# Memory attention and bilinear FFN: three groups of small-tile matmuls made neighbours, and the next-but-one batch's loads moved into the output stage

## The chip, the core and the metric

The kernel runs on one core of a Trainium2 chip. The metric is device time in microseconds (us). The kernel before takes 522.99 us (median of three runs, 522.94 to 523.03). Its profiled execution took 522.87 us, of which the span that the trace covers is 520.7 us. All times below, unless said otherwise, count from the start of that span.

## The reference

Eight batches, eight heads, 576 tokens, head dimension 64, 32 memories. `q` and `k` come multiplied by 200. Attention goes through the memories, and its output feeds a bilinear feed-forward network:

```python
a = phi - np.max(phi, axis=2, keepdims=True)          # max over the tokens
a = np.exp(a); a = a / (np.sum(a, axis=2, keepdims=True) + 1e-09)
k_m = np.einsum('bhsm,bhsd->bhmd', a, k)
v_m = np.einsum('bhsm,bhsd->bhmd', a, v)
scores = scale * np.matmul(q, k_m.transpose(0, 1, 3, 2))
scores = scores - np.max(scores, axis=-1, keepdims=True)
attn = np.exp(scores); attn = attn / (np.sum(attn, axis=-1, keepdims=True) + 1e-09)
x = np.matmul(attn, v_m)                               # heads side by side: 4608 x 512
h = (x @ w1) * (x @ w2) @ w3                           # 512 -> 1024 -> 1024
out = h @ w_out                                        # 1024 -> 512
```

## The kernel before, in words

Batch by batch (b = 0 to 7) the kernel works through a row of small steps. The order of all five engines is written out by hand: one token per step in three tables, `FIRST` for b = 0, `SECOND` for b = 1 and `BATCH` for b = 2 to 7. Each engine executes its share of the steps in the table's order and waits where data or a buffer isn't there yet; nothing overtakes on an engine. Two stages make up a batch: the a·b stage, with 16 units, and the out stage, with 14.

Tokens that matter here, with the line and the engine:

- `A`, `a`, `g`: one unit of a·b. `A` is 12 matmuls 128 x 288 on tiles 128\*128 (L596, TensorE = PE) into two PSUM banks of a ring of four ("ab" banks); `a` copies one bank (L605, ScalarE = ACT), `g` multiplies the other by it (L608, VectorE = DVE). fp32 values are split into a high and a low part, so each product is three matmuls.
- `M0` to `M3`: 16 matmuls each with 64\*32 tiles (L346) that multiply the values' memories into `w1` and `w2`; `Mh` (L357, ACT) and `Ml` (L365, DVE) split the result. M0 and M1 of batch b+1 are done in the out stage of b, M2 and M3 in the a·b stage of b+1.
- `phi`, `kv`, `q`: loads issued by SyncE (SP; L144 and L146, L154 and L160, L165). `phi` brings two tensors, `ph` (memories down the partitions, for the maximum) and `a` (tokens down the partitions).
- `top`: the maximum of `ph` (L185, DVE). `bm`: two transposes that spread it (L203, PE). `bs`: its subtraction from `a` (L208, L212, DVE). `be`: the exponential of `a` (L216, ACT). `mem`: the matmuls for k_m and v_m, 64 with 128\*32 tiles (L224) and 16 with 64\*32 tiles (L233). `exp`, `norm`, `memc`, `block`, `blockc`: sums and normalization (L191 to L261). In the a·b stage of batch b these are the steps of batch b+1.
- `sc0`, `sc1` (L274), `scc`, `mx`, `sb`, `ex`, `sm`, `mu`, `tr`, `ah`, `al`: scores and softmax of batch b+1 in two halves, its probabilities split in high and low.
- `O`: one of 14 units of the output (12 matmuls 128 x 288, L656); `h` and `l` split their operand (L635 on ACT, L641 on DVE); `S1` to `S4` and `f` sum operands on GpSimd (POOL; L622, L624, L626, L614); `p1`, `C11`, `C12` and so on keep and finish results (L672, L683), and each `C` issues a store (L668, SP).
- `W`: products of `w3` and `w_out`, eight matmuls 128 x 512 (L498); `C1` to `C5`: conversion of their float64 words. Both are in the first 130 us only.

A token with a minus sign is a step of batch b itself. `s_sb` (the scores) shares its buffer with `a` and `at` (the probabilities) shares one with `ph`, so `phi` of batch b+1 can only be loaded once batch b's softmax has let go of both: SP issues `kv` at the start of the a·b stage, `phi` 5.7 us later, and `q` in the out stage.

Of the kernel before, what the change touches and what calls it, by code (L numbers as in the profile page):

```python
# [25 lines left out]
C3 C2 C2 C3 C2 C2 C1 C4 C4 C5 C3 C4 C4 C1 C1 C5 C5 C1 C1 C3 C2 C3 C5 C1 C4 C2 C4 C3 C5 C2 C3 C1 C5 C2 C2 C1 C4 C5 C1  # L26
C4 C4 C3 C5 C3 C5 C1 C2 C3 C4 C5 C2 C1 C4 C3 C5 C1 C2 C3 C4 C5 phi0 kv0 C1 C2 C3 C4 C1 C2 q0 X0 X1 C3 C5 C4 C5 C1 C1
X2 W01 W02 W03 W04 W05 W06 W07 C2 C4 C3 C2 -top C2 C5 C4 -bm -bs -exp C3 C5 C1 C4 -norm W10 K3 Kh3 K1 Kh1 -be -mem C3
K0 -memc Kh0 -block Kt1 Kt0 Kt3 C5 -blockc C2 C3 r0 K2 r1 r3 s0 Kl1 Kt2 s3 C1 C4 C5 W11 -sc0 -sc1 -scc0 -scc1 -mx0
-sb0 C1 -mx1 -sb1 C3 C2 C1 C4 C5 -ex0 C3 C2 C4 C2 C5 -sm0 -mu0 -tr0 C3 C1 -ex1 C2 C1 C3 C4 C5 -sm1 C4 C5 C2 C2 -ah0  # L30
W12 W13 W14 W15 W16 M0 Mh0 M1 -mu1 -tr1 C1 -ah1 Mh1 W17 C3 -al0 Ml0 -al1 C4 Ml1 phi C4 Dt3 F3 Dt0 A a A g A C3 a C2 a
Et0 g C5 g C1 C5 A A a g Et3 t0 Kh2 Kl2 s1 a Dt2 C2 Dt1 g M2 Mh2 Ml2 C4 A A F0 f0 a C1 g a C3 r2 g top A A a C1 a C4
C5 g g C3 q kv C5 F1 F2 f1 f2 z0 A A D2 a a D3 w2 M3 Mh3 g Et2 E2 g Ml3 A A a w3 w1 a Kl3 s2 Kl0 y2 y1 E3 bm g g h2 h0
A A D0 a bs l2 g E0 f3 y3 S2 be mem A exp D1 a norm Et1 memc l0 E1 block w0 y0 g blockc O sc0 a t2 z2 g h1 h4 l1 t3 h3
t1 z3 z1 M0 scc0 mx0 l4 sb0 O Mh0 h6 l3 S3 S1 O O l6 h5 Ml0 l5 S4 O O h7 p1 h11 ex0 O p4 l7 h9 h8 C11 sm0 mu0 l8 tr0
# [783 lines left out]
```

## Time and profile before

| | us |
|---|---|
| runs, median of three | 522.99 (522.94 to 523.03) |
| profiled execution | 522.87 |
| its span | 520.7 |
| PE busy | 510.8 (98%) |
| DVE busy | 380.2 (73%) |
| ACT busy | 279.4 (54%) |
| POOL busy | 140.2 (27%) |
| period of a batch, b = 4 to 6 | 56.10 |

The profile counts an engine as busy while an instruction of it runs; matmuls overlap one another, so PE's progress is read from the starts of its instructions: a matmul of 288 columns starts every 0.132 us, a unit of 12 takes 1.59 us. A change of PE's work shows as a step between two starts that is longer than the usual one. The prediction speaks of three places: the warm stage (the first 50 us), the a·b stage and the out stage of a middle batch (b = 4 starts its a·b stage at 298.57, its out stage at 329.04; b = 5 starts at 354.67).

### The profile page before, as it was taken

The page shows a single profiled execution, that of the slowest core. Times are in us where ns is not written, and L with a number is a line of the kernel's source. Part 1 is how long each engine was busy: PE and PEld are TensorE (multiplying, and loading weights), DVE is VectorE, ACT ScalarE, POOL GpSimd, SP SyncE. Part 2 cuts the span into 40 slices and gives each one's busy share as a digit, 9 for nine tenths or more (in the row PEclk, how much of TensorE's full clock was granted, in tenths as well). Part 3 has the DMA queues.
Part 4 walks back from the last instruction along what each step waited for, and adds up shares of the span by engine and source line. Part 5 has one row for each costly group of instructions (what it writes and reads, how often), then busy time and mean ns, then how long its engine had stood idle before and what let it go on. Part 6 is the DMA issues. An engine that isn't in the chain of part 4 may idle for free.

```text
span 520.7 us, 10995 instructions
## 1 busy us (share of the span) xinstructions
PE 510.8 (98%) x4486; PEld 442.2 (85%) x4486; DVE 380.2 (73%) x655; ACT 279.4 (54%) x493; POOL 140.2 (27%) x158
## 2 busy tenths in 40 slices
...
GB/s 280 413 408 362 387 101 186 208 1 115 194 149 2 115 237 104 3 81 145 230 3 15 125 313 4 2 115 238 104 1 111 144 204 1 24 47 24 2 23 70
DMA packets 29794, 68.86 MB, mean 132 GB/s; under 512 B 1840, under 2 KB 10032, under 8 KB 29744
## 3 DMA queue, kind: packets, MB, share of 16 engines
...
q8 instruction: 35, 0.57, 0.5%
q14 instruction: 15, 0.12, 0.1%
...
## 4 chain that ended last, share of the span: by engine, by line
PE 86%; DMA 8%; ACT 2%; DVE 2%; issue 1%; SPq 0%; DVEq 0%; ACTq 0%
PE ab L596 36%; PE o L656 15%; PE x L656 15%; PE ab L656 5%; DMA raw<-in_w3T 3%; PE ab L346 3%; DMA q<-in_qT 3%; PE x L224 3%; DMA raw<-in_w_out 2%; PE o L498 2%; PE x L498 2%; PE ab L274 2%; PE o L346 1%; PE x L346 1%; DVE a L208 1%; ACT a L216 1%
## 5 line engine op out<-in xcount | busy, mean ns | idle before, releaser
L596 PE MATMUL ab<-ah,mh 128*128 128x288 f32 x512 | 154.5, 302 | 0.0
L596 PE MATMUL ab<-ah,ml 128*128 128x288 f32 x512 | 151.6, 296 | 0.0
L596 PE MATMUL ab<-al,mh 128*128 128x288 f32 x512 | 149.5, 292 | 0.0
L641 DVE TENSOR_TENSOR sl<-g,sh 128x576 fp32r<-128x576 f32 x112 | 89.3, 821 | 28.0 <-ACT sh L635 25.9
L635 ACT CAST sh<-g 128x576 fp32r<-128x576 f32 x112 | 75.2, 676 | 60.2 <-PE o L656 34.7
L596 PEld LDWEIGHTS ab<-ah,mh 128*128 128x128 f32 x512 | 96.2, 188 | 9.2 <-issue 7.3
L608 DVE TENSOR_TENSOR g<-ab,a_sb 128x288 f32<-128x288 f32 x128 | 57.7, 454 | 60.7 <-PE ab L596 46.3
L596 PEld LDWEIGHTS ab<-al,mh 128*128 128x128 f32 x512 | 97.4, 190 | 0.2 <-issue 0.2
L605 ACT COPY a_sb<-ab 128x288 f32<-128x288 f32 x128 | 51.2, 400 | 83.7 <-PE ab L596 80.9
L596 PEld LDWEIGHTS ab<-ah,ml 128*128 128x128 f32 x512 | 96.0, 188 | 0.0
L614 POOL TENSOR_TENSOR g<-g,g 128x288 f32<-128x288 f32 x32 | 26.0, 824 | 173.2 <-DVE g L608 173.2
L622 POOL TENSOR_TENSOR g<-g,g 128x288 f32<-128x288 f32 x32 | 29.4, 937 | 114.5 <-DVE sl L641 114.5
L656 PE MATMUL o<-sh,Wh 128*128 128x288 f32 x192 | 58.0, 302 | 0.0
L656 PE MATMUL x<-sh,Wl 128*128 128x288 f32 x192 | 56.6, 295 | 0.0
L656 PE MATMUL o<-sh,Wl 128*128 128x288 f32 x192 | 56.6, 295 | 0.0
L656 PE MATMUL x<-sl,Wh 128*128 128x288 f32 x192 | 56.6, 295 | 0.0
L656 PE MATMUL o<-sl,Wh 128*128 128x288 f32 x192 | 56.6, 295 | 0.0
L656 PE MATMUL x<-sh,Wh 128*128 128x288 f32 x192 | 56.4, 294 | 0.0
L656 PEld LDWEIGHTS o<-sh,Wh 128*128 128x128 f32 x192 | 36.1, 188 | 11.4 <-issue 5.5
L656 PEld LDWEIGHTS o<-sl,Wh 128*128 128x128 f32 x192 | 36.1, 188 | 0.0
L656 PEld LDWEIGHTS o<-sh,Wl 128*128 128x128 f32 x192 | 36.1, 188 | 0.0
L656 PEld LDWEIGHTS x<-sh,Wh 128*128 128x128 f32 x192 | 36.1, 188 | 0.0
...
## 6 DMA issues: line engine op xcount, KB each, us to landing
...
ph<-in_phiT SPq DMA_DIRECT2D x8, 576.0 KB, 6.6
a<-in_phi_tok SPq DMA_DIRECT2D x8, 576.0 KB, 7.8
...
```

The costliest lines, as they stand in the source:

```text
L224: nc.tensor.matmul(ps[t][h * M : (h + 1) * M, : 2 * D], lhsT=v["a"][:, (NT * i + t) * P + h * M : (NT * i + t) * P + (h + 1) * M], rhs=kvt ...
L274: nc.tensor.matmul(ps[t][g * M : (g + 1) * M], lhsT=km[b % 2][t * D : (t + 1) * D, g], rhs=v["q"][t * D : (t + 1) * D, g, n * HALF : (n + ...
L346: nc.tensor.matmul(ps[t][g * M : (g + 1) * M], lhsT=vm[b % 2][d, g], rhs=w12_sb[q][d, :, g], start=True, stop=True,)
L498: nc.tensor.matmul(pw[r][i][:, cols], lhsT=x[:, i * P : (i + 1) * P], rhs=wos[k // half][:, k % half, cols], start=k == 0 and cols.start == 0,
L596: nc.tensor.matmul(banks[w][:, :HALF], lhsT=x[:, t, w, fc : fc + P], rhs=y[:, n, t * HALF : (t + 1) * HALF], start=i == 0, stop=i == len(t ...
L605: nc.scalar.copy(out=a_sb, in_=banks[0][:, :HALF])
L608: nc.vector.tensor_tensor(out=G[n, f // half][:, f % half], in0=banks[1][:, :HALF], in1=a_sb, op=ALU.mult)
L614: nc.gpsimd.tensor_tensor(out=low, in0=top, in1=low, op=ALU.subtract)
L622: gp(out=s2, in0=s2, in1=s3, op=ALU.subtract)
L635: nc.scalar.copy(out=hi, in_=src)
L641: nc.vector.tensor_tensor(out=lo, in0=src, in1=hi.bitcast(F32), op=ALU.subtract)
L656: nc.tensor.matmul(ps[j][:, :HALF], lhsT=piece(x, s, 2 * part + k)[:, jc], rhs=y[:, k], start=i in (1, 4, 2, 5) and part == 0 and k == 0 a ...
```

## The change

M2, M3 and `mem` stand side by side in the a·b stage of batches 1 to 7, `mem` with its 64\*32 matmuls first; M3 goes to two ab banks in place of the pair "x". The loads of `kv`, `q` and `phi` of batch b+2 stand together in the out stage of batch b (from `SECOND` or `BATCH` on), behind the store of C11, and `top` of batch b+2 is the last step of the out stage. `s_sb` and `at` get buffers of their own. All three tables are written anew: in `FIRST`, `bm` stands between W06 and W07 where it was behind W07, and `phi` of batch 1 is loaded ahead of the last pieces of `w1` and `w2`; in `BATCH`, `h5` and `l5` stand ahead of `S4` on DVE and POOL after `S1`, and C11 stands behind `sm0`.

```diff
 SECOND = """
-A A M3 M2 a a g -mu1 g -tr1 -ah1 A A -al1 phi kv h0 a g a Mh3 g Mh2 Ml3 A a A a g A Ml2 a g g top A A a a bm g g bs A
+A A a a g g A a bm bs A a be M3 Mh3 g -mu1 -tr1 -ah1 -al1 Ml3 g M2 Mh2 exp mem A h1 a Ml2 g A a A a l1 g g A A a a g g
...
 BATCH = """
-A M2 M3 -mu1 Mh3 a -tr1 g A A -ah1 a a g -al1 g A A a a Mh2 h0 Ml3 kv phi g g A A a a g Ml2 A a top g A a h1 g g bm A
...
+A A a a g g A a bm bs A a be -mu1 g -tr1 -ah1 -al1 g M2 Mh2 M3 Mh3 mem A Ml3 a Ml2 g exp A A a a g g h0 A A a a norm g
...
+scc0 l6 mx0 sb0 M0 O O O p1 S3 h7 S1 h5 l5 S4 Mh0 O Ml0 l7 ex0 sm0 C11 O O M1 sc1 h8 mu0 p4 l8 h9 l9 h12 h10 Mh1 kv q
+phi tr0 O O l10 scc1 mx1 ah0 u2 h11 l11 l12 p5 h13 sb1 al0 l13 ex1 O O O O sm1 C22 Ml1 C21 C12 top
...
         def memories(bank):
             kvt = loaded.pop(("kv", b))
             ps = v["memories"] = bank()
+            for h in range(4):
+                for t in range(NT):
+                    nc.tensor.matmul(
+                        ps[t][h * M : (h + 1) * M, : 2 * D],
+                        lhsT=v["a"][t * D : (t + 1) * D, 4 * NT * P + h * M : 4 * NT * P + (h + 1) * M],
...
+                        start=True,
+                        stop=False,
+                    )
             for t in range(NT):
                 for i in range(4):
...
-                            start=i == 0,
-                            stop=False,
+                            start=False,
+                            stop=i == 3,
...
-                s_sb = att.tile([P, NT * S], F32, name="s_sb", tag="a")
+                s_sb = att.tile([P, NT * S], F32, name="s_sb", tag="s")
...
-                v["at"] = att.tile([P, 2, S], F32, name="at", tag="ph")
+                v["at"] = att.tile([P, 2, S], F32, name="at", tag="at")
...
-                        steps[at][what](pair_ab if b == 0 or not in_a else pair_x if digit == "3" else pair_o)
+                        steps[at][what](pair_ab if b == 0 or not in_a or digit == "3" else pair_o)
                 elif what in LOADS:
-                    load(what + ("1" if what == "phi" or in_a else "2"), b)
+                    load(what + ("1" if in_a else "2"), b)
...
-                    at = b if key[0] == "-" else b + 1
+                    at = b if key[0] == "-" else b + 2 if what == "top" and not in_a else b + 1
```

On PE, the a·b stage of a middle batch before the change: M2 and M3 (L346) stand between the first and the second unit, `mem` (L224, L233) later, between two other units (L596; `x`, `o` and `ab` are PSUM banks, `w_2` and `w_3` quarters of w1 and w2).

```order
L596 MATMUL ab<-ah,ml_3268 128x288
L346 MATMUL o<-w_2_80,vm_76 32x512 x8
L346 MATMUL x<-w_3_81,vm_76 32x512 x8
L596 MATMUL ab<-ah,mh_3265 128x288
...
L224 MATMUL x<-kv_3672,a 32x128 x8
L224 MATMUL x<-kv_3674,a 32x128 x8
...
L233 MATMUL x<-kv_3676,a 32x128 x8
L596 MATMUL ab<-ah,mh_3666 128x288
```

The same stage after it: `bm` (L203) two units into the merged group, then M2, M3 and `mem`.

```order
L203 MATMUL x<-ident,mx 128x128 x2
...
L346 MATMUL o<-w_2_80,vm_76 32x512 x8
L346 MATMUL ab<-w_3_81,vm_76 32x512 x8
L223 MATMUL x<-kv_3452,a 32x128 x8
L233 MATMUL x<-kv_3448,a 32x128 x8
L233 MATMUL x<-kv_3450,a 32x128 x8
...
L596 MATMUL ab<-ah,mh_3358 128x288
```

Units stood between M3 and `mem` and now none does; between `bm` and M2 there is one unit, where there were two between `bm` and `mem`.

On PE in the warm stage before: the four products W04 to W07 (L498 into ab), then `bm` of batch 0, then W10.

```order
L498 MATMUL ab<-wo_84,w_171 128x512 x8
L498 MATMUL ab<-wo_85,w_201 128x512 x8
L498 MATMUL ab<-wo_85,w_231 128x512 x8
L203 MATMUL x<-ident,mx 128x128 x2
L498 MATMUL o<-wo_84,w_290 128x512 x2
```

And after:

```order
L498 MATMUL ab<-wo_84,w_175 128x512 x8
L498 MATMUL ab<-wo_85,w_202 128x512 x8
L498 MATMUL ab<-wo_85,w_231 128x512 x4
L203 MATMUL x<-ident,mx 128x128 x2
L498 MATMUL ab<-wo_85,w_231 128x512 x4
```

`bm` moved ahead of the last product, W07 (the last four matmuls into ab).

On SP before, one batch: `q` in the out stage, its stores, then `kv`, `phi` and `a` at the start of the next batch's a·b stage.

```order
L668 DMA outT<-c 128x2x288
L165 DMA q<-in_qT 128x4x576
L668 DMA outT<-c 128x2x288 x3
L154 DMA kv_3672<-in_kv 128x2x1024
L154 DMA kv_3674<-in_kv 128x2x1024
L160 DMA kv_3676<-in_kv 64x512 x2
L144 DMA ph<-in_phiT 128x2x576
L146 DMA a<-in_phi_tok 128x1152
```

And after, from the store of C11 on:

```order
L668 DMA outT<-c_3340 128x2x288
L154 DMA kv0_3448<-in_kv 128x2x1024
L154 DMA kv2_3450<-in_kv 128x2x1024
L160 DMA kv4_3452<-in_kv 64x512 x2
L165 DMA q_3455<-in_qT 128x4x576
L144 DMA ph_3457<-in_phiT 128x2x576
L146 DMA a_3459<-in_phi_tok 128x1152
L668 DMA outT<-c_3505 128x2x288
```

All loads now follow C11's store; `q` stands ahead of `ph`, and the other three stores behind `a`.

## Rows read from the trace of the kernel before

**Rows 1.** The page's first part: the span, then busy time (share of the span) and number of instructions of PE and the other engines.

```profile
span 520.7 us, 10995 instructions
PE 510.8 (98%) x4486; PEld 442.2 (85%) x4486; DVE 380.2 (73%) x655; ACT 279.4 (54%) x493; POOL 140.2 (27%) x158
```

**Rows 2.** Busy time by stretch, one period of a batch (b = 4), with PE's granted clock (PEclk, 1.00 is full) at the end.

```profile
298.57:354.67 56.10, 56.05 (x543) 51.51 (x542) 40.56 (x71) 26.58 (x51) 14.44 (x16) 1.00 0.32 107
```

**Rows 3.** The chain of work that ended last, in order of time (start us, us, what): the transfer it starts with before 50 us, and a stretch of units.

```profile
34.05 15.60 DMA q<-in_qT
...
302.18 12.90 PE ab L596 x96
```

**Rows 4.** Timeline of PE around M2 and M3 of batch 4: start us, us, line, operation, tile size, columns, count. The first row is the last matmul of the unit before, the last the first matmul of the unit behind.

```profile
300.01 0.29 PE L596 MATMUL ab<-ah,ml 128*128 128x288 f32 x1
300.24 1.09 PE L346 MATMUL o<-w,vm 64*32 64x512 f32 x16
301.12 1.06 PE L346 MATMUL x<-w,vm 64*32 64x512 f32 x16
302.11 0.40 PE L596 MATMUL ab<-ah,mh 128*128 128x288 f32 x1
```

**Rows 5.** Timeline of PE from `bm` to behind `mem` in the same batch, and last ACT's row for `be` in that stretch.

```profile
314.90 0.38 PE L203 MATMUL x<-ident,mx 128*128 128x128 f32 x2
...
318.17 0.29 PE L596 MATMUL ab<-ah,ml 128*128 128x288 f32 x1
318.51 1.95 PE L224 MATMUL x<-kv,a 128*32 128x128 f32 x64
320.39 0.45 PE L233 MATMUL x<-kv,a 64*32 64x128 f32 x16
320.77 0.40 PE L596 MATMUL ab<-ah,mh 128*128 128x288 f32 x1
321.01 0.29 PE L596 MATMUL ab<-al,mh 128*128 128x288 f32 x1
...
317.29 1.17 ACT L216 ACTIVATE a<-a 128x1152 f32<-128x1152 f32 x1 [0.77 <-DVE a L212]
```

**Rows 6.** Timeline of PE in the warm stage, with the idle time before an instruction and what ended it in brackets; the last row is DVE's `top` there.

```profile
24.42 14.00 PE L498 MATMUL ab<-wo,w 128*128 128x512 f32 x32 [0.57 <-DVE wo L487]
38.25 0.38 PE L203 MATMUL x<-ident,mx 128*128 128x128 f32 x2
38.47 1.88 PE L498 MATMUL o<-wo,w 128*128 128x512 f32 x4
...
42.74 1.99 PE L224 MATMUL ab<-kv,a 128*32 128x128 f32 x64 [0.25 <-ACT a L216]
...
45.62 0.58 PE L254 MATMUL ab<-ident,kvm 128*128 128x128 f32 x2 [0.51 <-ACT kvm L245]
46.04 1.88 PE L498 MATMUL o<-wo,w 128*128 128x512 f32 x4
...
49.78 0.60 PE L274 MATMUL ab<-q,km 64*32 64x288 f32 x8
...
35.56 1.35 DVE L185 TENSOR_REDUCE mx<-ph 128x2 f32<-128x1152 f32 x1 [3.29 <-DMA ph<-in_phiT]
```

**Rows 7.** Timeline of SP: the issues of `kv` (two of its four transfers), `ph` and `a` at the start of batch 3 (243.89 to 250.03), and of `kv` and `a` at the start of batch 4 (299.98, 306.11); the last row is the three stores ahead of `kv` of the batch after. Start us, us to issue.

```profile
243.89 1.01 SPq L154 DMA_DIRECT2D kv<-in_kv  x2
...
249.62 0.37 SPq L144 DMA_DIRECT2D ph<-in_phiT  x1
250.03 0.47 SPq L146 DMA_DIRECT2D a<-in_phi_tok  x1
...
299.98 1.00 SPq L154 DMA_DIRECT2D kv<-in_kv  x2
...
306.11 0.47 SPq L146 DMA_DIRECT2D a<-in_phi_tok  x1
...
352.60 3.43 SPq L668 DMA_DIRECT2D outT<-c  x3
```

**Rows 8.** DMA issues of the same two stretches: size of one in KB, and us from issue to landing. The first two rows are batch 3's `ph` and `a`, the last is batch 4's `a`.

```profile
ph<-in_phiT SPq DMA_DIRECT2D x1, 576.0 KB, 6.2
a<-in_phi_tok SPq DMA_DIRECT2D x1, 576.0 KB, 7.1
...
a<-in_phi_tok SPq DMA_DIRECT2D x1, 576.0 KB, 8.0
```

**Rows 9.** Timeline of DVE in the out stage of batch 4: `Ml0` (two halves), the second half of C11, the first of `sm0`'s three instructions, and C12, the last result.

```profile
333.01 1.29 DVE L365 TENSOR_TENSOR ml<-ab,mh 128x512 fp32r<-128x512 f32 x2 [0.85 <-ACT mh L357]
...
340.46 0.46 DVE L683 TENSOR_TENSOR c<-ab,c 128x288 f32<-128x288 f32 x1 [0.34 <-PE ab L656]
340.84 0.75 DVE L303 TENSOR_REDUCE ss<-s_sb 128x18 f32<-128x576 f32 x1
...
354.87 0.76 DVE L683 TENSOR_TENSOR c<-x,c 128x576 f32<-128x576 f32 x1 [0.44 <-PE x L656]
```

**Rows 10.** Timeline of DVE and POOL in the same stage: a low part (L641) and a subtraction (L295) of the same size on DVE, and the four instructions of a step `S` on POOL that run beside them.

```profile
337.38 0.74 DVE L641 TENSOR_TENSOR sl<-g,sh 128x576 fp32r<-128x576 f32 x1
338.05 1.36 DVE L295 TENSOR_TENSOR s_sb<-s_sb,st 128x576 f32<-128x576 f32 x1
...
337.43 4.19 POOL L626 TENSOR_TENSOR g<-g,g 128x288 f32<-128x288 f32 x4
```

More of the change, by code (lines that the diff above doesn't have):

```diff
@@ L25 @@
 FIRST = """
[L26 to L35, printed above, removed]
@@ L36 @@
-l9 M1 sc1 q O O O h10 ah0 l10 u2 p5 h13 h12 Mh1 scc1 l11 mx1 l12 l13 al0 sb1 Ml1 ex1 O O O O C12 C21 C22 sm1
+C3 C2 C2 C3 C2 C1 C1 C4 C5 C3 C4 C4 C5 C1 C5 C1 C2 C3 C2 C1 C4 C4 C5 C1 C3 C2 C5 C1 C3 C3 C4 C5 C2 C2 C4 C1 C4 C2 C2
+C4 C5 C1 C3 C4 C5 C3 C5 C1 C1 C3 C2 C5 C3 C2 C4 C1 C4 C3 C5 C5 phi0 kv0 C1 C2 C3 C2 q0 X0 X2 X1 W01 C1 C3 C4 C4 C5 C5
+W02 W03 W04 W05 W06 C2 C4 C1 C3 C1 C5 -top -bm W07 C1 -bs W10 C2 C3 C4 C2 -exp K1 K0 Kh0 C3 K2 Kh2 Kt1 Kt0 r0 -be -mem
+Kh1 Kl1 C4 C5 -norm C5 r1 -memc phi -block C1 -blockc C2 C3 K3 C2 C3 Kh3 C4 C5 W11 -sc0 -sc1 -scc0 -scc1 -mx1 C1 -sb1
@@ new lines @@
+C2 C3 C2 C4 C5 -mx0 C1 C1 C3 -ex1 -sb0 -ex0 C4 C4 C5 C2 C1 C5 C3 C1 C2 C2 -sm1 -mu1 -sm0 -mu0 C4 C5 W12 W13 W14 W15
+W16 M0 Mh0 -tr0 C4 -ah0 C4 -tr1 M1 Mh1 W17 -al0 Ml0 Ml1 A A Kl2 s1 Kt2 s0 Kt3 C3 C5 Kl0 C1 -ah1 -al1 r3 a a C3 D2 Dt0
+F0 Dt3 g A a Et0 g C5 g Kl3 f0 A A C2 t0 a Et3 g a C2 M2 Mh2 C4 Dt1 Dt2 F2 s3 F1 g A a Ml2 E2 Et2 g C4 A C3 t3 a g top
+F3 f2 A A C1 q a g C5 C3 a g C1 C5 kv z0 A A D3 a a E3 w0 f1 w3 y3 y0 w2 M3 Mh3 g Et1 t1 D0 g Ml3 bm A A a g bs z1 a
+w1 D1 g E1 h2 f3 y1 h1 l1 be l2 S2 A A exp a mem E0 norm h0 l0 a memc r2 h4 y2 z3 s2 A g g block blockc O O O l4 phi
@@ L37 @@
+h6 t2 z2 a g h3 l6 l3 sc0 M0 h5 scc0 l5 S3 S1 S4 O O h10 Mh0 p1 h7 top mx0 sb0 l7 Ml0 O C11 O O h11 h8 ex0 h9 p4 l8
+sc1 scc1 l9 l10 sm0 M1 O u2 Mh1 h12 O O kv q l12 l11 h13 p5 mu0 mx1 tr0 l13 ah0 al0 O O O sb1 C21 Ml1 ex1 sm1 C12 C22
 """
 SECOND = """
-A A M3 M2 a a g -mu1 g -tr1 -ah1 A A -al1 phi kv h0 a g a Mh3 g Mh2 Ml3 A a A a g A Ml2 a g g top A A a a bm g g bs A
-A a be mem exp a g g l0 norm A A h4 a memc block a g h2 h1 g blockc l2 A a g A A a a l4 l1 O g g h3 l3 sc0 M0 scc0 mx0
-sb0 O O O O f3 f0 f1 S2 p1 h6 l6 h5 l5 O O f2 S3 S1 S4 ex0 Mh0 sm0 C11 Ml0 h7 h9 h10 p4 h8 l7 l8 mu0 sc1 M1 Mh1 l9 q O
```

23 lines of the change are left out of this document (8 added, 15 removed).

## The prediction

> **What bounds the kernel now.** I read the page's busy shares first. PE is busy 510.8 of 520.7 us, 98%, DVE 73% [rows 1]. The busy times by stretch come next: in the period of batch 4 PE is busy 56.05 of 56.10 us at a granted clock of 1.00 [rows 2], so a batch takes what its matmuls take and no faster clock is to be had. The chain of waits shows the only other thing: up to 49.65 us it is a transfer, `q` of batch 0 [rows 3], and from the first scores at 49.78 [rows 6] it follows PE to the end. So two things change the time: the starts of PE's instructions (a step longer than usual is lost time), and any wait of PE that the new order brings. Whatever delays PE after 49.78 us is paid in full, since no later idle time can absorb it. The timeline of PE shows the first; the timelines of DVE, SP and POOL, with the new order beside them, show the second.
>
> **The merged visit.** A matmul of a unit starts 0.134 us after the one before (12.90 / 96 [rows 3]). Into M2 the step is 0.23 (300.01 to 300.24), 0.10 too long. M2 takes 0.88 (to 301.12), M3, the same 16 matmuls, 0.99 (to 302.11): 0.11 for leaving the small tiles [rows 4]. The first matmul of the unit behind `mem` takes 0.24 (320.77 to 321.01), again 0.11 too long [rows 5], and I take the same behind M3, whose last row shows the same lengthened matmul (0.40). Into `mem` the step is 0.34 (318.17 to 318.51), 0.21 too long; part of this is a wait for `be`, which ends at 317.29 + 1.17 = 318.46 [rows 5]. Side by side, M3's way out (0.11 + 0.11) and `mem`'s way in (0.21) fall away: 0.43 per batch. The way into M2, the change between 64\*32 and 128\*32 inside `mem`, and the way out remain. Does `be` still end in time? Before, `mem` starts 3.61 us behind `bm` (314.90 to 318.51 [rows 5]); after, between them stand `bm` 0.14, one unit 1.70, the way in 0.10, M2 and M3 0.88 each: 3.70. So hardly any wait is left. Six batches (1 to 6) merge, batch 7 has no `mem`, batch 0 stays apart: 6 x 0.43 = 2.6 us gained. Lower bound: going from M3 to `mem` costs as much as the way in from a unit did, 6 x 0.22 = 1.3. Upper bound: the first inner change goes as well, 6 x 0.47 = 2.8. I take 2.6, because M3's tiles and `mem`'s first 16 matmuls have the same shape, and between matmuls of one shape no long step shows.
>
> **The warm stage.** The new place of `bm` makes PE wait for `top`. `top` runs 35.56 to 36.91 and starts when `ph` lands [rows 6]; loads stand in the same order up to it, so it can't start sooner. PE runs W04 to W07 without a gap, 13.83 us for four (24.42 to 38.25), so W06 ends at 34.8. Before, W07 filled the time; now PE is idle from 34.8 to 36.95, 2.1 us. From there: `bm` 0.22, W07 and W10 3.45 each, `mem` at 44.1, which then waits for nothing (before, it started at 42.74 after waiting). From `mem` to `block` 2.88 with its wait for `memc`, `block` 0.42 (45.62 to 46.04), W11 3.45: done at 50.9, against 49.65 when `q` is there. `sc0` moves from 49.78 to 51.0: 1.25 lost. Waits that the old order had (0.25 before `mem`, some in W10, 0.13 for `q`) are what the 2.1 shrinks by. Bounds: 1.0, if `memc`'s wait of 0.51 also shrinks; 1.8, if ACT, whose order there has changed, brings `be` late again.
>
> The loads of the late `w1` and `w2` pieces come some 3 us later, since `ph` and `a` of batch 1 go ahead. Their conversions run on DVE and ACT with more than that to spare before M2 and M3 need them; I cost this at nothing, with 0.5 us if the cover is gone.
>
> **The loads in the out stage.** This is the uncertain term. The kernel before has `ph` in time for its `top`; now `top` is DVE's last step of the out stage, behind C12 (354.87 + 0.76 [rows 9]) and ahead of the next batch's first `g`. If `ph` isn't there, DVE stands still, and behind it the `g` that frees banks, `bm` and `bs`. PE needs DVE's first `g` (0.46) done when it starts its fourth unit, 3 x 1.59 + 0.14 = 4.9 us into the batch. With `top` 1.35 that leaves 4.9 - 1.35 - 0.46 = 3.1: `ph` must land 3.1 us into the batch.
>
> When does it land? SP issues `kv` behind C11's store. In the new order C11 comes on DVE behind `l5` (ends about 9.6 us into the out stage), `Ml0` 1.29, `l7` 0.74, `sm0` about 1.2 (its first instruction takes 0.75) and takes 2 x 0.46 itself [rows 9, 10]: about 13.6, and `kv` is issued at about 14.0 (the out stage starts at 329.04, the next batch at 354.67, so 11.6 us before the batch). The time allowed from `kv`'s issue to `ph`'s landing is 11.6 + 3.1 = 14.7 us. The nearest rows: in batch 3 `a` lands at 250.03 + 7.1 = 257.13, 13.24 us behind `kv`'s issue at 243.89; in batch 4 at 306.11 + 8.0 = 314.11, 14.13 behind 299.98 [rows 7, 8]. By then `kv`, `ph` and `a` are in, 2304 + 576 + 576 KB. The new order has `kv`, `q` and `ph`: 2304 + 1152 + 576, one transfer of 576 KB more. Batch 3's `a` lands 1.31 behind its `ph` (249.62 + 6.2 = 255.82). So 14.55 to 15.44 against 14.7 allowed: 0.15 to spare, or 0.74 late. Four batches (3 to 6) do this. I take 0.25 each, 1.0 us, nearer the early end: before, three stores go out in the 3.4 us ahead of `kv` [rows 7], after only one. Bounds: nothing, and 1.1 each (4.4 us), if DVE also passes C11 0.3 later.
>
> In a sentence of its own: the Trainium skill, page "DMA: Bandwidth & Descriptors", section "Two DMAs through the same engine are not ordered", says that within one queue of a DMA engine descriptors start in order; by it `q`'s 1152 KB lie ahead of `ph` whichever is needed first. The landings above agree (`ph` 1.31 ahead of `a`, in the order of issue).
>
> **Steps costed at nothing.** M3 in ab banks: four half-size instructions in place of two on ACT and DVE, which are busy under three quarters of the time [rows 1]. Buffers of their own for `s_sb` and `at`: only waits go. `mem`'s other order: the same 80 matmuls.
>
> **Sum.** -2.6 + 1.25 + 1.0 = -0.35 us. On the profiled execution (span 520.7, time 522.87) that is 522.5; the median of the runs is 0.12 above it, so 522.6. A measurement of this kernel can tell 0.2% from no change, 1.05 us: faster begins at 521.94, slower at 524.04.
>
> **Rivals.**
> First, `ph` lands in time everywhere: -2.6 + 1.25 = -1.35, 521.6. For it: batch 3's row has 0.15 to spare. Against: batch 4's hasn't. With the warm stage at its lower bound, 521.4.
>
> Second, the other side: `ph` decides. From 14.7 us between `kv`'s issue and its landing on, each us more costs PE one in four batches. At batch 4's row with C11 a little later it is 1.1 us each: 522.6 - 1.0 + 4.4 = 526.0. For it: two stages that were apart now share one queue within one stage. Against: batch 3's row.
>
> Third, `l5` loses time to POOL. On DVE the subtraction at 338.05 took 1.36, the low part before it, of the same size, 0.74; POOL's `S` ran from 337.43 in four instructions of 1.05 each [rows 10]. In the new order `l5` (0.74) comes about 8.8 us into the out stage, when POOL goes from `S1` to `S4`, and PE needs it at 9.9: 0.3 to spare. If it takes the 1.36 and a wait of the same size, it is some 0.45 late, in batches 2 to 6: 5 x 0.45 = 2.2, 524.8. The Trainium skill, page "SBUF — State Buffer", section "SBUF: two separate sides", calls the ports that DVE and GpSimd share an exclusive lock: whoever starts first has it for the whole instruction and the other blocks. By that rule it is all or nothing, one POOL instruction or none; the row of 1.36 agrees, being 0.62 longer than the free one. Against the rival: `l5` may start in front of POOL's next instruction.
>
> Fourth, the merge gives its lower bound: 522.6 + 1.3 = 523.9.
>
> **Chances.** Forecast (521.9 to 523.4) 0.38; `ph` in time 0.26; `ph` late 0.16; `l5` 0.12; small merge 0.08. Faster: the case in time and a small part of the forecast, with part of the merge's upper bound in it, 0.36. Within 0.2%: most of the forecast and the small merge, 0.37. Slower: the late case, `l5` and what the two give in part, 0.27. The range of 8 in 10 leaves out the far end of the late case and the best of the early one: 521.1 to 525.0.
>
> **What would show it.** In the profile of the changed kernel: the rows of M2, M3 and `mem` should follow at 0.88, 0.88 and then `mem`'s 16 without a step over 0.15. In the warm stage PE should be idle about 2 us before `bm`, released by DVE's `top`, and `sc0` should start near 51.0. In batches 3 to 6 DVE's `top` should be idle before it on `ph`'s landing; if that idle time ends later than 3.1 us into the batch, PE's fourth unit starts late by as much. PE's rows before the tenth microsecond of the out stage tell of `l5`. The forecast is wrong if the period of a middle batch isn't between 55.67 (56.10 - 0.43) and 56.4, or if `sc0` doesn't move.

## The result and the profile after

The changed kernel takes 527.72 us (median of six runs, 525.77 to 530.29), the kernel before in the same comparison 522.97 (522.90 to 523.04). The ratio is 1.0088 with a 95% interval of 1.0058 to 1.0117: slower, where 522.6 was forecast and the range ended at 525.0. In this comparison the kernel before repeats within 0.14 us, the changed one within 4.5; in the later comparisons the kernel before itself ranges over 1.7 to 1.9. One run of the kernel before in those, 561.39 us at a granted clock of 0.85, is left out of every figure.

The page of the changed kernel, parts 1 and 4 (answering to [rows 1] and [rows 3]): PE's share of the span is a point lower at the same busy time, and in the chain transfers have nearly twice their old share. Part 4 of the kernel before stands below it.

```profile
span 525.5 us, 11026 instructions
...
PE 511.1 (97%) x4486; PEld 443.4 (84%) x4486; DVE 381.1 (73%) x662; ACT 282.6 (54%) x500; POOL 142.5 (27%) x158
...
PE 72%; DMA 15%; DVE 5%; SPq 3%; ACT 2%; issue 1%; POOL 0%; DVEq 0%; POOLq 0%; ACTq 0%
```

```profile
PE 86%; DMA 8%; ACT 2%; DVE 2%; issue 1%; SPq 0%; DVEq 0%; ACTq 0%
```

Where the time went is read best from the starts of the stages, the first matmul of each in PE's timeline (us). From batch 1 on the rows are the starts of the out stages, so that each stretch holds one visit to the small tiles in the a·b stage (a visit is a stay on tiles other than 128\*128 between two units). "Step" is what the stretch ahead of the row added or saved:

| start of | before | after | difference | step |
|---|---|---|---|---|
| a·b stage, batch 0 | 73.41 | 74.42 | +1.01 | +1.01 |
| out stage, batch 0 | 104.57 | 107.04 | +2.47 | +1.45 |
| out stage, batch 1 | 160.75 | 162.78 | +2.03 | -0.44 |
| out stage, batch 2 | 216.86 | 218.43 | +1.57 | -0.46 |
| out stage, batch 3 | 272.94 | 275.49 | +2.54 | +0.97 |
| out stage, batch 4 | 329.04 | 331.65 | +2.62 | +0.07 |
| out stage, batch 5 | 385.14 | 388.89 | +3.75 | +1.13 |
| out stage, batch 6 | 441.24 | 445.85 | +4.62 | +0.87 |
| out stage, batch 7 | 494.31 | 498.95 | +4.64 | +0.03 |
| end of span | 520.65 | 525.54 | +4.88 | +0.24 |

Batches 1 and 2, the ones without a wait, gain 0.44 and 0.46. Batches 3 to 6 merge in the same way and yet lose time: against -0.44 each they are 1.41, 0.51, 1.57 and 1.31 us too long, 4.8 in all. The waits of PE name the cause (line waited with, what for: us in total, times, longest):

```profile
PE x L203 <- DVE mx L185: 5.4, 5, 1.8
...
PE ab L596 <- DVE g L608: 0.7, 1, 0.7
PE x L223 <- DMA kv<-in_kv: 0.4, 1, 0.4
```

`bm` (L203) waits for `top` five times; the longest, 1.8, is the warm stage, the other four are batches 3 to 6. PE's timeline of batch 5 (its a·b stage starts at 357.28) shows such a wait and the merged visit behind it, answering to [rows 4] and [rows 5]:

```profile
361.91 0.29 PE L596 MATMUL ab<-ah,ml 128*128 128x288 f32 x1
363.47 0.40 PE L203 MATMUL x<-ident,mx 128*128 128x128 f32 x2 [1.27 <-DVE mx L185]
363.75 0.40 PE L596 MATMUL ab<-ah,mh 128*128 128x288 f32 x1
...
365.30 0.29 PE L596 MATMUL ab<-ah,ml 128*128 128x288 f32 x1
365.53 1.09 PE L346 MATMUL o<-w,vm 64*32 64x512 f32 x16
366.41 1.06 PE L346 MATMUL ab<-w,vm 64*32 64x512 f32 x16
367.27 0.42 PE L223 MATMUL x<-kv,a 64*32 64x128 f32 x16
367.62 1.96 PE L233 MATMUL x<-kv,a 128*32 128x128 f32 x64
369.51 0.40 PE L596 MATMUL ab<-ah,mh 128*128 128x288 f32 x1
369.75 0.30 PE L596 MATMUL ab<-al,mh 128*128 128x288 f32 x1
```

From 361.91 to 363.47 PE starts no matmul. The visit itself is as forecast: M2 0.88, M3 0.86 (it was 0.99), no step in front of `mem`, 0.24 for the first unit behind. DVE's timeline of that time says why `top` is late (answering to [rows 9]; first the steps ahead of C11, then the end of the out stage):

```profile
342.36 0.95 DVE L641 TENSOR_TENSOR sl<-g,sh 128x576 fp32r<-128x576 f32 x1
343.23 0.74 DVE L303 TENSOR_REDUCE ss<-s_sb 128x18 f32<-128x576 f32 x1
344.00 0.77 DVE L304 TENSOR_SCALAR ss<-ss 128x18 f32<-128x18 f32 x1
...
344.99 0.76 DVE L683 TENSOR_TENSOR c<-ab,c 128x288 f32<-128x288 f32 x2
...
357.52 0.74 DVE L683 TENSOR_TENSOR c<-x,c 128x576 f32<-128x576 f32 x1
361.98 1.35 DVE L185 TENSOR_REDUCE mx<-ph 128x2 f32<-128x1152 f32 x1 [3.72 <-DMA ph<-in_phiT]
363.25 0.81 DVE L608 TENSOR_TENSOR g<-ab,a_sb 128x288 f32<-128x288 f32 x2
```

DVE is done with C12 at 358.26 and stands for 3.72 us until `ph` is there. SP's timeline has the issues, and the list of DMA issues of the stretch (KB, us to landing) gives `ph` its landing at 349.23 + 12.7 = 361.9 (answering to [rows 7] and [rows 8]):

```profile
345.81 0.37 SPq L668 DMA_DIRECT2D outT<-c  x1
346.27 0.96 SPq L154 DMA_DIRECT2D kv<-in_kv  x2
...
348.64 0.54 SPq L165 DMA_DIRECT2D q<-in_qT  x1
349.23 1.20 SPq L144 DMA_DIRECT2D ph<-in_phiT  x1
```

```profile
q<-in_qT SPq DMA_DIRECT2D x1, 1152.0 KB, 11.4
ph<-in_phiT SPq DMA_DIRECT2D x1, 576.0 KB, 12.7
```

`kv` goes out 14.62 us into the out stage (346.27 - 331.65), 11.0 ahead of the next batch, and `ph` lands 15.7 behind it: 4.7 us into a batch that can bear 3.1. `top` starts 4.51, 3.62, 4.70 and 4.42 us into batches 3 to 6, and each of these, less 3.1, is that batch's loss to within 0.03 us.

The other large losses are both in batch 0. The warm stage, PE's timeline (answering to [rows 6]):

```profile
37.10 0.40 PE L203 MATMUL x<-ident,mx 128*128 128x128 f32 x2 [1.80 <-DVE mx L185]
...
44.39 0.45 PE L223 MATMUL ab<-kv,a 64*32 64x128 f32 x16
...
50.91 1.20 PE L274 MATMUL ab<-q,km 64*32 64x288 f32 x32
```

`sc0` starts at 50.91, it was 49.78. And 1.45 us are lost in batch 0's a·b stage, of which the forecast knew nothing. PE's fourth unit there starts 0.99 behind the matmul before it, 0.86 too long: it waits for a `g`, and that stands on DVE behind a step of the output weights (L561, `Dt3`) that itself waits for POOL. Most of the rest is the last wait of the list above, 0.4 us of `mem` for `kv` of batch 1. The timelines of PE and of DVE:

```profile
79.46 0.29 PE L596 MATMUL ab<-ah,ml 128*128 128x288 f32 x1
80.45 0.40 PE L596 MATMUL ab<-ah,mh 128*128 128x288 f32 x1 [0.70 <-DVE g L608]
```

```profile
77.14 0.41 DVE L561 TENSOR_TENSOR sl<-o,raw 128x256 f32<-128x256 f32 x1
79.61 0.42 DVE L561 TENSOR_TENSOR sl<-x,raw 128x256 f32<-128x256 f32 x1 [2.06 <-POOL Wl L521]
79.95 0.45 DVE L608 TENSOR_TENSOR g<-ab,a_sb 128x288 f32<-128x288 f32 x1
```

The 0.24 at the end of the table comes from one place too: in batch 7's out stage PE's first matmul on a low part (`l5`, DVE 506.07 to 507.29) starts at 507.35, 0.33 behind the one before.

### The profile page after: what moved, and what is told of

It reads as the page before. It is cut to its first block, busy times and chain, and to the rows that moved or that the text cites. A ratio compares the mean times of both kernels' runs of the same rounds, so it can differ in the third digit from the quotient of the medians.

```text
span 525.5 us, 11026 instructions
## 1 busy us (share of the span) xinstructions
PE 511.1 (97%) x4486; PEld 443.4 (84%) x4486; DVE 381.1 (73%) x662; ACT 282.6 (54%) x500; POOL 142.5 (27%) x158
## 4 chain that ended last, share of the span: by engine, by line
PE 72%; DMA 15%; DVE 5%; SPq 3%; ACT 2%; issue 1%; POOL 0%; DVEq 0%; POOLq 0%; ACTq 0%
PE ab L596 32%; DMA ph<-in_phiT 12%; PE o L656 10%; PE x L656 10%; PE ab L346 4%; PE ab L656 3%; PE o L498 3%; PE x L498 3%; PE x L233 3%; DMA raw<-in_w_out 2%; DMA kv<-in_kv 2%; PE ab L274 1%; PE o L346 1%; DVE mx L185 1%; SPq L419 1%
## 5 line engine op out<-in xcount | busy, mean ns | idle before, releaser
L596 PE MATMUL ab<-ah,mh 128*128 128x288 f32 x512 | 153.0, 299 | 0.7 <-DVE g L608 0.7
L596 PE MATMUL ab<-al,mh 128*128 128x288 f32 x512 | 151.1, 295 | 0.0
L596 PE MATMUL ab<-ah,ml 128*128 128x288 f32 x512 | 151.0, 295 | 0.0
L641 DVE TENSOR_TENSOR sl<-g,sh 128x576 fp32r<-128x576 f32 x112 | 91.3, 834 | 12.6 <-ACT sh L635 12.4
L596 PEld LDWEIGHTS ab<-ah,mh 128*128 128x128 f32 x512 | 96.3, 188 | 4.7 <-issue 1.3
L596 PEld LDWEIGHTS ab<-al,mh 128*128 128x128 f32 x512 | 96.3, 188 | 0.2 <-issue 0.2
L596 PEld LDWEIGHTS ab<-ah,ml 128*128 128x128 f32 x512 | 96.3, 188 | 0.0
L614 POOL TENSOR_TENSOR g<-g,g 128x288 f32<-128x288 f32 x32 | 27.7, 896 | 218.3 <-DVE g L608 218.3
L656 PE MATMUL x<-sh,Wh 128*128 128x288 f32 x192 | 57.8, 301 | 0.0
L656 PE MATMUL o<-sh,Wh 128*128 128x288 f32 x192 | 56.5, 294 | 0.0
L622 POOL TENSOR_TENSOR g<-g,g 128x288 f32<-128x288 f32 x32 | 25.8, 828 | 76.2 <-DVE sl L641 76.2
L656 PEld LDWEIGHTS x<-sl,Wh 128*128 128x128 f32 x192 | 36.1, 188 | 0.0
```

The source lines that it names most:

```text
L596: nc.tensor.matmul(banks[w][:, :HALF], lhsT=x[:, t, w, fc : fc + P], rhs=y[:, n, t * HALF : (t + 1) * HALF], start=i == 0, stop=i == len(t ...
L614: nc.gpsimd.tensor_tensor(out=low, in0=top, in1=low, op=ALU.subtract)
L622: gp(out=s2, in0=s2, in1=s3, op=ALU.subtract)
L641: nc.vector.tensor_tensor(out=lo, in0=src, in1=hi.bitcast(F32), op=ALU.subtract)
L656: nc.tensor.matmul(ps[j][:, :HALF], lhsT=piece(x, s, 2 * part + k)[:, jc], rhs=y[:, k], start=i in (1, 4, 2, 5) and part == 0 and k == 0 a ...
```

## The experiments

In the comparisons below the kernel before ran at 522.81 to 522.94 (medians), its runs between 521.6 and 523.9. The first 73 us of a kernel differ from profile to profile: in the eight profiles that have the changed kernel's order there, the first unit of a·b starts anywhere from 73.19 to 75.92. Seven of these have its order of batch 0's a·b stage too, and that stage adds 1.09 to 1.48 in them. The steps of the later batches repeat within 0.02 us in kernels with the same tables for them. So beside each time stands the step of the batches against the kernel before, worked out as in the table above; the kernel before has one profile.

**Is it the landing of `ph`, or `top`'s place on DVE?** Two runs change nothing but the order in which SP issues.

```diff
-scc0 l6 mx0 sb0 M0 O O O p1 S3 h7 S1 h5 l5 S4 Mh0 O Ml0 l7 ex0 sm0 C11 O O M1 sc1 h8 mu0 p4 l8 h9 l9 h12 h10 Mh1 kv q
-phi tr0 O O l10 scc1 mx1 ah0 u2 h11 l11 l12 p5 h13 sb1 al0 l13 ex1 O O O O sm1 C22 Ml1 C21 C12 top
+scc0 l6 mx0 sb0 M0 O O O p1 S3 h7 S1 h5 l5 S4 Mh0 O Ml0 l7 ex0 sm0 C11 O O M1 sc1 h8 mu0 p4 l8 h9 l9 h12 h10 Mh1 kv phi
+q tr0 O O l10 scc1 mx1 ah0 u2 h11 l11 l12 p5 h13 sb1 al0 l13 ex1 O O O O sm1 C22 Ml1 C21 C12 top
```

> The changed kernel with one edit: in the table of batches 2 to 7 the load of phi is issued ahead of q (kv, phi, q). Theory A (ph lands too late, and DVE's top holds PE in batches 3 to 6): ph lands some 3 us sooner, the four waits of bm for top (1.25, 0.36, 1.43 and 1.16 us of idle in the profile of the changed kernel, 4.8 us by batch periods) go, 527.7 - 4.8 = 522.9 us, and the runs agree within 0.3 us again. Theory B (it is top's place behind C12 and ahead of the first g, 1.35 us of DVE, that holds PE, whenever ph lands): no change, 526.5 or more.

522.13 us, ratio 0.9983 (0.9974 to 0.9993): 5.6 us under the changed kernel, and faster than before. All six merged batches now step by -0.43 to -0.46. DVE's timeline at the start of batch 5 (353.77):

```profile
354.00 0.75 DVE L683 TENSOR_TENSOR c<-x,c 128x576 f32<-128x576 f32 x1
354.67 1.34 DVE L185 TENSOR_REDUCE mx<-ph 128x2 f32<-128x1152 f32 x1
355.93 0.45 DVE L608 TENSOR_TENSOR g<-ab,a_sb 128x288 f32<-128x288 f32 x1
```

`top` starts straight behind C12 and PE doesn't notice its 1.34 us. (In batches 3 and 6 it still waits for `ph`, 0.6 and 0.9 us, and PE loses nothing there either.) Theory B is out: the place is good as long as the data is there. The runs still spread over 1.5 us (521.27 to 522.74), but so does the kernel before in this comparison (522.14 to 523.80).

```diff
-scc0 l6 mx0 sb0 M0 O O O p1 S3 h7 S1 h5 l5 S4 Mh0 O Ml0 l7 ex0 sm0 C11 O O M1 sc1 h8 mu0 p4 l8 h9 l9 h12 h10 Mh1 kv q
-phi tr0 O O l10 scc1 mx1 ah0 u2 h11 l11 l12 p5 h13 sb1 al0 l13 ex1 O O O O sm1 C22 Ml1 C21 C12 top
+scc0 l6 mx0 sb0 M0 O O O p1 S3 h7 S1 h5 l5 S4 Mh0 O Ml0 l7 ex0 sm0 C11 O O M1 sc1 h8 mu0 p4 l8 h9 l9 h12 h10 Mh1 phi kv
+q tr0 O O l10 scc1 mx1 ah0 u2 h11 l11 l12 p5 h13 sb1 al0 l13 ex1 O O O O sm1 C22 Ml1 C21 C12 top
```

> The changed kernel with phi issued first of the three loads (phi, kv, q) in batches 2 to 7. Theory A: ph lands 10 us before it is needed, so the time is that of the order kv, phi, q within 0.3 us, about 522.9. If the order kv, phi, q still leaves ph partly late, this one is faster by what is left. Theory B: 526.5 or more.

522.06 us (521.40 to 522.45), ratio 0.9984 (0.9975 to 0.9993), the same steps. More lead than the order kv, phi, q gives buys nothing. This kernel, "phi first", is the base of most runs below.

**Would an earlier issue have done?** The changed kernel with its own order of loads, C11 two steps sooner:

```diff
-scc0 l6 mx0 sb0 M0 O O O p1 S3 h7 S1 h5 l5 S4 Mh0 O Ml0 l7 ex0 sm0 C11 O O M1 sc1 h8 mu0 p4 l8 h9 l9 h12 h10 Mh1 kv q
+scc0 l6 mx0 sb0 M0 O O O p1 S3 h7 S1 h5 l5 S4 Mh0 O Ml0 l7 C11 ex0 sm0 O O M1 sc1 h8 mu0 p4 l8 h9 l9 h12 h10 Mh1 kv q
```

> The changed kernel, its loads in its own order (kv, q, phi), with C11 put ahead of ex0 and sm0 in batches 2 to 7, so that its store and the loads behind it are issued sooner. Theory (the landing of ph decides, us for us): kv is issued 1.2 to 1.8 us sooner, and each of the four waits of bm shrinks by as much: of 1.25, 0.36, 1.43 and 1.16 at most 0.3 us each is left, some 523.0 us. If the transfers only get slower in the earlier place: 525 or more.

522.15 us, ratio 0.9993 (0.9982 to 1.0005). All four waits are gone, the steps are -0.43 to -0.45. `top` still waits for `ph` and no longer for long; DVE's timeline at the start of batch 5 (354.60):

```profile
354.79 0.76 DVE L683 TENSOR_TENSOR c<-x,c 128x576 f32<-128x576 f32 x1 [0.23 <-PE x L656]
357.07 1.35 DVE L185 TENSOR_REDUCE mx<-ph 128x2 f32<-128x1152 f32 x1 [1.52 <-DMA ph<-in_phiT]
```

`kv` goes out 12.91 us into the out stage, 1.71 sooner. `ph` is there 2.5 us into the batch, 2.95 in batch 6, the latest of the four, within the 3.1 that the forecast allowed, and PE loses nothing. One step of 1.8 us on DVE, `sm0`, decided over 5 us of the kernel.

**What is a visit to the small tiles worth?** Two runs that set out to part the merged visit in two failed as tests, and tell something else.

```diff
-A A a a g g A a bm bs A a be -mu1 g -tr1 -ah1 -al1 g M2 Mh2 M3 Mh3 mem A Ml3 a Ml2 g exp A A a a g g h0 A A a a norm g
+A A a a g g A a bm bs A a be -mu1 g -tr1 -ah1 -al1 g M2 Mh2 M3 Mh3 A mem Ml3 a Ml2 g exp A A a a g g h0 A A a a norm g
```

> The kernel with phi first, and one unit of a*b put between M3 and mem in batches 2 to 6 (five visits made apart again). If side by side saves what the forecast says, 0.43 us each: 2.1 us slower than phi first, some 525.0. If the small tiles cost the same wherever they stand: the same time as phi first.

532.22 us, a step of +1.63 to +1.66 in batches 2 to 6. And with the unit between M2 and M3:

```diff
-A A a a g g A a bm bs A a be -mu1 g -tr1 -ah1 -al1 g M2 Mh2 M3 Mh3 mem A Ml3 a Ml2 g exp A A a a g g h0 A A a a norm g
+A A a a g g A a bm bs A a be -mu1 g -tr1 -ah1 -al1 g M2 Mh2 A M3 Mh3 mem Ml3 a Ml2 g exp A A a a g g h0 A A a a norm g
```

> The kernel with phi first, and one unit of a*b put between M2 and M3 in batches 2 to 6, so that M3 and mem still stand together and no bank is held longer. If each way out of and into the small tiles costs what the rows of before show (0.22 and 0.10 us): five more, 1.6 us slower than phi first, 523.7. If a visit costs nothing of itself: the same time.

542.74 us, steps of +2.49 to +4.07. PE's timeline shows what that unit does:

```profile
313.86 1.09 PE L346 MATMUL o<-w,vm 64*32 64x512 f32 x16
...
316.81 0.40 PE L596 MATMUL ab<-ah,mh 128*128 128x288 f32 x1 [1.86 <-ACT ah L318]
```

The fifth unit is the first that needs the second half of the probabilities (`ah1`, `al1`), which DVE and ACT finish only now. The merged visit covers that time; a unit moved ahead of it waits. PE's list of waits has the two, for `ah` and for `al`, five times each in both runs, and in the list of the changed kernel they don't stand. So both times say what a wrong place costs. The clean test leaves the units in place and moves M2 instead:

```diff
-A A a a g g A a bm bs A a be -mu1 g -tr1 -ah1 -al1 g M2 Mh2 M3 Mh3 mem A Ml3 a Ml2 g exp A A a a g g h0 A A a a norm g
+A A a a g g A a bm bs M2 A a be -mu1 g -tr1 -ah1 -al1 g Mh2 M3 Mh3 mem A Ml3 a Ml2 g exp A A a a g g h0 A A a a norm g
```

> The kernel with phi first, and M2 put one unit earlier in batches 2 to 6, behind bm, so that one unit stands between M2 and M3 and no unit moves ahead of the probabilities that it needs (as one did in the two runs that set out to part the visit). One more way out (0.22) and in (0.10) per batch: the step of batches 2 to 6 against the kernel before is -0.12 in place of -0.44, 1.6 us slower than phi first. If a visit costs nothing of itself: -0.44.

523.96 us, 1.9 above phi first; the step is -0.10 to -0.13 in batches 2 to 6. The table serves batch 7 as well, whose step goes from +0.04 to +0.38: six visits more, not five, some 2.0 us in all. PE's timeline of batch 4 (the profiled execution is the slowest of the ten, 526.01, and lies 2.51 behind already at the first unit, ahead of the part that was changed):

```profile
306.75 1.09 PE L346 MATMUL o<-w,vm 64*32 64x512 f32 x16
...
307.77 0.40 PE L596 MATMUL ab<-ah,mh 128*128 128x288 f32 x1
308.01 0.29 PE L596 MATMUL ab<-al,mh 128*128 128x288 f32 x1
...
309.56 1.09 PE L346 MATMUL ab<-w,vm 64*32 64x512 f32 x16
```

M2 takes 1.02 with its way out (0.88 in a merged visit) and the first matmul behind it 0.24: the price of one visit more is 0.33, 0.32 was expected. `mem`'s inner order, put back:

```diff
-            for h in range(4):
-                for t in range(NT):
...
-                        start=True,
-                        stop=False,
-                    )
             for t in range(NT):
                 for i in range(4):
...
-                            start=False,
-                            stop=i == 3,
+                            start=i == 0,
+                            stop=False,
                         )
+            for h in range(4):
+                for t in range(NT):
...
+                        start=False,
+                        stop=True,
+                    )
```

> The kernel with phi first, and mem's matmuls in the order of the kernel before (64 on 128*32 tiles first, the 16 on 64*32 tiles last), so that M3 and mem's first matmuls have different tiles. If each change of tile size has its price: one more change per merged visit, some 0.11 us in six visits, 0.7 us slower than phi first, and a batch's step against the kernel before is -0.33 in place of -0.44 us. If only the way from and to 128*128 tiles counts: -0.44 as it was.

522.68 us; the steps are -0.27 to -0.29. PE's timeline of batch 4:

```profile
306.83 1.06 PE L346 MATMUL ab<-w,vm 64*32 64x512 f32 x16
307.82 1.95 PE L224 MATMUL x<-kv,a 128*32 128x128 f32 x64
309.70 0.45 PE L233 MATMUL x<-kv,a 64*32 64x128 f32 x16
```

M3 takes 0.99 again where 64\*32 is followed by 128\*32. So a third of the gain of a merged visit, 0.16 of 0.44, is that equal tiles stand side by side, more than the 0.11 expected; 0.13 of it is M3's (0.99 against 0.86).

**The losses of batch 0.** First the whole of `FIRST` from the kernel before, on phi first, with the new loads added:

```diff
-l9 M1 sc1 q O O O h10 ah0 l10 u2 p5 h13 h12 Mh1 scc1 l11 mx1 l12 l13 al0 sb1 Ml1 ex1 O O O O C12 C21 C22 sm1
+l9 M1 sc1 kv phi q O O O h10 ah0 l10 u2 p5 h13 h12 Mh1 scc1 l11 mx1 l12 l13 al0 sb1 Ml1 ex1 O O O O C12 C21 C22 sm1 top
```

> The kernel with phi first, and the whole order of batch 0 (the warm stage and batch 0's own stages) taken back from the kernel before, with only the loads and top of batch 2 added to its out stage. Theory: all that is lost up to the out stage of batch 0 (0.4 us by the first unit of a*b, 1.5 more in batch 0's a*b stage, in the profile of phi first) comes from the new order of batch 0; it goes, and the six merged visits (0.44 each by that profile) stay: 522.1 - 1.9 = 520.2 us. Rival: the loss comes from what is common to both (mem's new inner order, buffers of their own, late kv of batch 1) and stays: about 522.

521.00 us, ratio 0.9964 (0.9951 to 0.9977). In its profile the first unit comes at +0.21, which the spread of the first 73 us doesn't tell from the others, and batch 0's a·b stage adds 0.03, where the seven profiles of the new order add 1.09 to 1.48: that loss is the new order of batch 0. The time is 0.8 above what was expected; batch 1, whose table was written for the other `FIRST`, gains 0.26 in place of 0.44, and the rest is within the spread. Then the single steps:

```diff
-F0 Dt3 g A a Et0 g C5 g Kl3 f0 A A C2 t0 a Et3 g a C2 M2 Mh2 C4 Dt1 Dt2 F2 s3 F1 g A a Ml2 E2 Et2 g C4 A C3 t3 a g top
+F0 g A a Et0 g Dt3 C5 g Kl3 f0 A A C2 t0 a Et3 g a C2 M2 Mh2 C4 Dt1 Dt2 F2 s3 F1 g A a Ml2 E2 Et2 g C4 A C3 t3 a g top
```

> The kernel with phi first; in batch 0 one subtraction of the output weights on DVE (Dt3, L561), which waits about 2 us for POOL, is put behind the first two g. Theory: PE's wait of 0.87 us ahead of its fourth unit of batch 0 is this one: it goes, some 0.8 us faster than phi first, 521.3. Rival: the wait passes to the next step that needs POOL, under 0.3 us.

520.75 us, ratio 0.9964 (0.9951 to 0.9977), with the last run below the fastest of all, and more than expected: batch 0's a·b stage adds 0.00 in place of 1.48. The step of 1.00 at the fourth unit, which every profile with `Dt3` ahead of the first `g` in the new order has, is gone. DVE's timeline:

```profile
77.79 0.45 DVE L608 TENSOR_TENSOR g<-ab,a_sb 128x288 f32<-128x288 f32 x1
79.07 0.42 DVE L561 TENSOR_TENSOR sl<-x,raw 128x256 f32<-128x256 f32 x1 [0.83 <-ACT Wh L517]
79.41 1.22 DVE L487 CUSTOM_DVE_ANT_0 w<-w,uw 128x2048 uint16<-128x2048 uint16 x1
```

The second `g` ends at 78.24 (in the changed kernel the first ended at 80.40), and the conversion behind it starts 1.6 us sooner (there 81.01). `mem`'s wait for `kv` of batch 1 is gone from PE's waits too; whether by this edit is not shown, since the first of these runs (kv, phi, q), with batch 0 unchanged, doesn't have it either.

```diff
-Kh1 Kl1 C4 C5 -norm C5 r1 -memc phi -block C1 -blockc C2 C3 K3 C2 C3 Kh3 C4 C5 W11 -sc0 -sc1 -scc0 -scc1 -mx1 C1 -sb1
+Kh1 Kl1 C4 C5 -norm C5 r1 -memc -block C1 -blockc C2 C3 K3 C2 C3 Kh3 C4 C5 W11 -sc0 -sc1 -scc0 -scc1 -mx1 C1 -sb1
...
-W16 M0 Mh0 -tr0 C4 -ah0 C4 -tr1 M1 Mh1 W17 -al0 Ml0 Ml1 A A Kl2 s1 Kt2 s0 Kt3 C3 C5 Kl0 C1 -ah1 -al1 r3 a a C3 D2 Dt0
+W16 M0 Mh0 -tr0 C4 -ah0 C4 -tr1 M1 Mh1 W17 -al0 Ml0 Ml1 phi A A Kl2 s1 Kt2 s0 Kt3 C3 C5 Kl0 C1 -ah1 -al1 r3 a a C3 D2 Dt0
```

> The kernel with phi first; phi of batch 1 is loaded behind the late pieces of w1 and w2 again, as before the change. Theory: kv of batch 1 lands some 3 us sooner, mem of batch 1 no longer waits for it (0.3 to 0.5 us): some 0.4 us faster than phi first, 521.7. Rival: top and bm of batch 1 then wait for ph: no gain or slower.

521.92 us, 0.1 under phi first: not to be told apart. In its profile batch 0's a·b stage adds 0.98 in place of 1.48, and `mem` doesn't wait for `kv`, as expected; but in the run kv, phi, q, where this load is unmoved, `mem` doesn't wait either and the stage adds 1.09. So the run doesn't tell what the place of the load is worth. The stage ahead came 0.56 later, within the spread.

```diff
-W02 W03 W04 W05 W06 C2 C4 C1 C3 C1 C5 -top -bm W07 C1 -bs W10 C2 C3 C4 C2 -exp K1 K0 Kh0 C3 K2 Kh2 Kt1 Kt0 r0 -be -mem
+W02 W03 W04 W05 W06 C2 C4 C1 C3 C1 C5 -top W07 C1 -bm -bs W10 C2 C3 C4 C2 -exp K1 K0 Kh0 C3 K2 Kh2 Kt1 Kt0 r0 -be -mem
```

> The kernel with phi first, and bm of batch 0 put behind W07 again. If the 2 us of idle time in front of bm are lost for good: sc0 comes back from 50.9 to about 49.8 us, 1.1 us faster than phi first, 521.8. Rival: the time is set by be or memc there, which follow bm, and mem then waits for them: 0 to 0.5 us faster.

521.56 us, 0.5 under phi first, but not where it was looked for: the first unit starts at +0.39 in both, and batch 0's a·b stage adds 0.96 in place of 1.48. There `mem` doesn't wait for `kv`, as in other runs whose `bm` wasn't moved, so the 0.5 can't be put down to `bm`. PE's timeline shows where the wait went:

```profile
43.50 0.72 PE L223 MATMUL ab<-kv,a 64*32 64x128 f32 x16 [0.75 <-ACT Wh L517]
```

`mem` now waits. `be` ends at 43.08 there, and the first half of `kv4`, the last transfer, which `mem`'s new order needs first, lands at 43.4 (issued at 26.17, 17.2 us to landing), just ahead of `mem`. The last run asks what `kv4` costs beside `be`: on top of Dt3 and `bm`, `mem` of batch 0 alone goes back to its old order.

```diff
+            full = [(h, t, i) for t in range(NT) for i in range(4) for h in range(4)]
+            rest = [(h, t, 4) for h in range(4) for t in range(NT)]
+            order = [full, rest] if b == 0 else [rest, full]
...
```

> Phi first, Dt3 behind the first two g, bm of batch 0 behind W07, and mem of batch 0 alone in the order of before (its last transfer, kv4, is then needed last). With bm alone moved back, the wait passed to mem (1.3 us), whose first matmuls need kv4. If that order is why nothing was won there: the first unit of a*b comes within 0.1 us of the kernel before's, and the time is 0.4 us under Dt3 alone, 520.4. If ACT's new order (be behind four copies and casts) is why: no gain, 520.8.

520.77 us, no gain over Dt3 alone. The timelines of PE and ACT (a line of code fell away, so L232 is `mem`):

```profile
43.32 2.33 PE L232 MATMUL ab<-kv,a 128*32 128x128 f32 x80 [0.91 <-ACT a L216]
```

```profile
42.11 1.16 ACT L216 ACTIVATE a<-a 128x1152 f32<-128x1152 f32 x1
```

`be` starts at 42.11 where it started at 41.53, behind one copy and one cast more, and `mem` starts straight behind its end. So the wait in front of `bm` was not lost time by itself: with `bm` moved back `mem` waits, first for `kv4`, and with `kv4` out of the way for `be`, which ACT's new order brings later. The first unit starts at +0.22 here and at +0.45 with Dt3 alone, too close to tell apart in this stretch.

## Why the prediction was wrong, point by point

**The merged visit: right.** Forecast 0.43 per batch and 2.6 in all; 0.44 and 2.66 (six steps of -0.44) measured once `ph` is there in time. The two prices behind it hold as well: 0.33 for one more way out and in, where the rows gave 0.32, and equal tiles side by side cost no step. Even the small wait of `mem` for `be` went, as worked out.

**The warm stage: right in this profile, which is partly luck.** 1.25 forecast, 1.13 at `sc0` and 1.01 at the first unit, with PE waiting 1.80 for `top` as described. But in the eight profiles with this order of the stretch that wait is 0.57 to 1.98 and `sc0` starts between 49.62 and 52.41; their median, 50.33, is 0.55 behind the kernel before's one profile. Moving `bm` back doesn't win even that for certain, since `kv4` and `be` then hold `mem`. That ACT brings `be` late again, which the forecast named as its upper bound, is part of how the stage works.

**The loads in the out stage: the step that failed.** The mechanism was described with its place, its four batches and the 3.1 us that a batch can bear, and the traces confirm that bound (`top` at 2.95 costs nothing with C11 sooner, at 3.62 it costs 0.5, at 4.7 it costs 1.6). The size was off: 0.25 each was taken, 1.2 on average measured, 4.8 for 1.0. Two numbers did it. `kv` was to be issued 14.0 us into the out stage and was issued at 14.62 in all four batches. On DVE, steps ahead of C11 ran longer beside POOL's sums than in the rows they were taken from: `l7` 0.95 for 0.74, and `sm0`'s second instruction 0.77 for 0.18 in the same batch's second half. And `ph` landed 14.6 to 15.7 us behind `kv`, 15.3 on average, where 14.55 to 15.44 were worked out and 0.25 late meant 14.95, on the ground that fewer stores go ahead. Three of the four landed near the late end or past it with one store ahead, so that ground is not borne out. The two together, 0.62 and 0.35, are the whole miss per batch. The balance of -0.35 could bear 0.34 late in each batch; at the late end (0.74 each) the sum would have been +1.6.

**The second rival came true.** It was priced at 526.0 and given 0.16; the median is 527.7, of which 1.45 are batch 0's own. (Its 1.1 each is 0.74 + 0.3, which makes 1.04, and 525.8 in all.) The range of 8 in 10 stopped at 525.0, short of a case that it held for possible.

**Batch 0's a·b stage: a term put at nothing.** The forecast has no term for DVE's new order there; its 0.5 stood for late pieces of `w1` and `w2`. 1.45 were lost: 0.86 by a wait on DVE for POOL that stands ahead of two `g`, which goes when `Dt3` is moved, and most of the rest by `mem`'s wait for `kv` of batch 1, which comes and goes between runs of the same order (0.4 here, none with kv, phi, q).

**The third rival, `l5` against POOL, did not happen in the batches it was named for.** In batch 4 `l5` takes 0.76 at 340.48, and with `ph` early the steps of batches 1 to 6 leave no room for such a loss. In batch 7 it did happen: `l5` took 1.22 there while POOL was summing, PE waited for it, and the 0.24 at the end of the span comes from this; every run here loses 0.22 to 0.25 there. The Trainium skill, page "SBUF — State Buffer", section "SBUF: two separate sides", says that of the instructions that need the ports DVE and GpSimd share, the one that starts first has them until it ends. The steps ahead of C11 agree: `l7` started at 342.36 inside a POOL instruction (341.87, 0.82 long) and took 0.21 more than alone, and `sm0`'s second instruction, started at 344.00 inside the last one (343.94, 0.80 long), ended with it.
